# A decode-attention kernel: shorter TensorE program with hardware loops, z built by GpSimd, head sums by one masked product

## Chip, cores, metric

One core of one Trainium2 chip. The metric is the device time of one execution in microseconds; times quoted are medians of several runs. A span is the stretch from the first to the last instruction. It is 1.3 to 1.6 us shorter than the time in most of them and up to 2.8 us shorter in a few, so a single high time need not come from the kernel's own work.

## The reference, cut to what matters

Two token rows go through grouped-query attention on a long cache, a small gated feed-forward part, and an output projection:

```
x = layernorm(A_x)                                  # (2, 1, 512)
q = (x @ wq)                                        # 32 query heads of 128
p = softmax(q . k_cache * 128**-0.5)                # cache: 2 x 8 kv heads x 32768 x 128, bf16
s = (p . v_cache) @ wo                              # 4 query heads share a kv head
g = silu(mlp(x))                                    # weights w3, w4: 1.8 MB each
out = A_x + s * g
```

K and V are 268 MB of the 280.5 MB that are read, each byte once. A *group* below is one of the 16 pairs (batch row, kv head): 8.39 MB of K and as much of V. *z* is the small tile that holds a group's query heads among zeros; it is the stationary operand of the score products. *Heads* are a group's finished, normalized results.

## The kernel before

Loads go through one queue, in order (in the trace of before the seven pieces of the output weights are issued from 610.3 to 613.2 us, and land one after the other from 642.7 to 650.1 us). K of the next group is released when the first half of this group's scores is done, V when its weighted sum is done. Both signals come from one-column marker matmuls (`mark`) on TensorE.

```python
    with pe.Fori(0, NG):
        head_sums()                       # of the group before
        take(pe, s_z)
        for i in range(NPART):            # two halves, written out
            for r in range(NR):
                take(pe, s_t)             # transposed K from VectorE
                ... 4 matmuls of 512 columns into sc[i] ...
                mm.then_inc(s_tf if r < NR - 1 else s_sc, 1)
            mark(s_tf)
            if i == 0:
                mark(p_k)                 # releases the next K load
        ... sum of the exponentials ...
        for h in range(NPART):            # weighted sum of V, half by half
            take(pe, s_v[h], 16)
            ... 32 matmuls, four at a time (at 63.2 us of the trace four start within 0.01 us) ...
        mm.then_inc(s_o, 1)
        mark(p_o)                         # releases the next V load
```

The weighted sum lies in PSUM as 4 blocks of 128 columns, each valid for some rows. ScalarE copies it (`ob`), TensorE adds up the right rows, VectorE normalizes and picks the diagonal:

```python
        act.copy(out=ob[:, :], in_=o[:, :]).then_inc(s_ob, 1)
        ...
        for t in range(VT):               # head_sums: 4 products of 128 columns, fp32
            mm = pe.matmul(oT, lhsT=sel_o[:, t, ...], rhs=ob[:, t * Dh:(t + 1) * Dh], ...)
        ...
        dve.reciprocal(rec, S); dve.scalar_tensor_tensor(xm, oT, rec, mask); dve.tensor_reduce(...)   # cut
```

At the end the output weights come in seven pieces behind the last V. Rows of the first two pieces do not need the last heads (`early`), and their sum is copied out by ScalarE while the last heads are still being made:

```python
    early(0)
    head_sums()
    k_e = P(early(1))
    k_es = A(act.copy(out=e_sb[:, :], in_=e_ps[:, :]))
    pe.wait_ge(s_r, NG + 2)               # the last heads
    product(2)
    ... four products that add the early sums ...
    for i in range(3, len(WO_PARTS)):
        mm = product(i)
```

The softmax here doesn't subtract the row's maximum and nothing guards it: scores larger than these inputs give would overflow.

Of the kernel before, what the change touches and what calls it, by code (L numbers as in the profile page):

```python
# [15 lines left out]
RT = 16  # L16
# [5 lines left out]
WO_PARTS = [(0, 0, 8), (0, 8, 16), (1, 0, 8), (1, 8, 12), (1, 12, 14), (1, 14, 15), (1, 15, 16)]  # L22
# [38 lines left out]
def kernel(  # L61
# [63 lines left out]
    xm = sbuf([128, WL, RS], F32, "xm")  # L125
# [5 lines left out]
    sel_t = sbuf([128, VT, rep], F32, "sel_t")  # L131
    sel_o = sbuf([128, VT, NQ, rep, WL], F32, "sel_o")
    sel_u = sbuf([128, rep], F32, "sel_u")
    sel_h = sbuf([128, NQ, rep, WL], F32, "sel_h")
    mask = sbuf([128, WL], F32, "mask")
    x_bf = sbuf([128, D], BF16, "x_bf")
    xf, xn, ln2 = (Ts[0].bitcast(F32)[:, 0:D], Ts[0].bitcast(F32)[:, D:2 * D], Ts[1].bitcast(F32)[:, 0:D])
    xn_bf = sbuf([128, D], BF16, "xn_bf")
    ln2_bf = sbuf([128, D], BF16, "ln2_bf")
# [20 lines left out]
    banks = [nc.alloc_psum_tensor(f"bank{i}", [128, 512], F32) for i in range(8)]  # L160
    sc = banks[0:2]
    o, S_b, oT_b, h_ps, treg_b, s_b = banks[2:8]
    S = S_b[:, 0:1]
    oT = oT_b[:, 0:Dh]
    treg = treg_b[:, 0:2 * DK * 16].bitcast(BF16)
    h2, e_ps = o, sc[0]
    e_sb = Ts[2].bitcast(F32)[:, 0:D]
    mark_ps = treg_b[0:1, 0:1]
# [13 lines left out]
    end_p, end_v = pe.alloc_register("end_p"), dve.alloc_register("end_v")  # L182
    for eng, reg in ((pe, end_p), (dve, end_v)):
        eng.reg_mov(reg, 0)
    s_far = nc.alloc_semaphore("s_far")
    ahead = pe.mark_branch_hint_location()
    top = nc.cur_bb
    pe.br_lt(end_p, 0, on_true="late", on_false="go").branch_hint(ahead)
    nc.switch_bb("go")
    hint_p, hint_v = pe.mark_branch_hint_location(), dve.mark_branch_hint_location()  # L190
    hints = [i.name for i in top.bb.instructions if isinstance(i, mybir.InstBranchHint)]
    begin(nc, first.ins.name, *hints)
# [6 lines left out]
    s_t, s_tf, s_z, s_sc, s_e, s_p, s_o, s_ob, s_x, s_on, s_d, s_r, p_k, p_o = (  # L199
        nc.alloc_semaphore(n)  # L200
        for n in ("s_t", "s_tf", "s_z", "s_sc", "s_e", "s_p", "s_o", "s_ob", "s_x", "s_on", "s_d", "s_r", "p_k",
                  "p_o")
# [49 lines left out]

    k_x0 = V(dve.memset(x_bf[:, :], 0.0))
# [9 lines left out]
    k_id = G(  # L263
# [4 lines left out]
    )  # L268
    G(pool.memset(ones_f[:, :], 1.0))
# [9 lines left out]
    V(dve.memset(s_ps, 0.0))  # L279
    V(dve.memset(o[:, :], 0.0))  # L280
    V(dve.memset(S, 1.0))
    V(dve.memset(oX[:, :], 0.0))
    V(dve.memset(h_bf[:, :, :], 0.0))
    k_t0 = V(dve.memset(xT[:, :, :], 0.0))
# [25 lines left out]
    k_xb = V(dve.tensor_copy(out=xn_bf[0:BW, :], in_=xn[0:BW, :]))  # L310
    k_l2 = layernorm(1, ln2, xn, k_xn)
    wait(dve, k_l2)
    k_lb = V(dve.tensor_copy(out=ln2_bf[0:BW, :], in_=ln2[0:BW, :]))
# [9 lines left out]
    wait(pe, k_id)  # L323
    for s, (src, k_src) in enumerate(((xn_bf, k_xb), (ln2_bf, k_lb))):
        wait(pe, k_src)
        for k in range(DK):
            c = (s * DK + k) * 32
            k_tr = P(pe.transpose(out=treg[:, c:c + BW], in_=src[0:BW, k::DK], identity=ident[0:BW, 0:BW]))  # L328

    wait(dve, k_id)  # L330
    V(
        dve.tensor_reduce(
            out=sel_t[:, :, :],
            in_=ident[:, :].rearrange("p (j a t h) -> p a t h j", j=4, t=VT, h=rep)[:, 0, :, :, :],
            axis=AX.X, op=ALU.add,
# [9 lines left out]
            out=mask[:, :], in_=ident[:, :].rearrange("p (j w) -> p w j", w=WL), axis=AX.X, op=ALU.add  # L345
# [9 lines left out]
    wait(dve, k_tr, k_t0)  # L355
    k_xT = V(
        dve.tensor_copy(out=xT[:, :, 0:B], in_=treg.rearrange("p (k c) -> p k c", c=32)[:, :, 0:BW:BS])
    )

    wait(pool, k_sh, (g_, g_.n))  # L360
    G(pool.tensor_copy(out=sel_h[:, :, :, :], in_=wide(sel_u[:, :], WL)))
    for t in range(VT):
        wait(pool, (g_, g_.n))
        G(pool.tensor_copy(out=sel_o[:, t, :, :, :], in_=wide(sel_t[:, t, :], WL)))
# [9 lines left out]
    for t in range(NQB):  # L374
        for k in range(DK):
            for n in range(NQ):
                c = (t * NQ + n) * GW
                i = pe.matmul(
                    sc[t][32 * n:32 * n + 32, :], lhsT=xT[:, k, :],
                    rhs=wq3[:, k, c:c + GW].rearrange("p (h w e) -> p h e w", h=rep * NB, e=2),  # L380
                    start=(k == 0), stop=(k == DK - 1), tile_position=(0, 32 * n),
                )
        k_q.append(P(i))
# [9 lines left out]
    def spread(eng, j, n):  # L393
        return (eng.copy if eng is act else eng.tensor_copy)(
            out=qr[32 * j:32 * j + 32, :, :, :].rearrange("p a e (m n h) -> p (a e) m n h", n=NQ, h=rep)[
                :, :, :, n, :
            ],
            in_=qT[32 * n:32 * n + 32, 0:B, :].rearrange("p b (t h a) -> p a (b t) h", t=NQB, h=rep),
        )

    wait(act, k_qT)
    wait(pool, k_qT, (g_, g_.n))
    for n in range(NQ):
        for j in range(NQ):
            if n < 2 or j < 2:
                k_qa = A(spread(act, j, n))
            else:
                k_qg = G(spread(pool, j, n))
# [3 lines left out]
    w4v = w34[:, W4O:W4O + FK * D].rearrange("p (f d) -> p f d", f=FK)  # L412
    HW = 32 * FK
    wait(pe, k_w3)
    for k in range(DK):
        for n in range(NQ):
            i = pe.matmul(
                h_ps[32 * n:32 * n + 32, 0:HW], lhsT=xT[:, DK + k, :], rhs=w3v[:, k, n * HW:(n + 1) * HW],
                start=(k == 0), stop=(k == DK - 1), tile_position=(0, 32 * n),
            )  # L420
    k_h = P(i)
    wait(dve, k_h)
    k = V(
        dve.transpose(
            out=hT[:, :, :], in_=h_ps[:, 0:HW].rearrange("p (q f) -> p f q", f=FK),
        )
    )
    hf = hT[:, :, 0:B]
# [19 lines left out]
    k_hb = V(dve.tensor_mul(out=h_bf[:, :, 0:BW:BS], in0=hf, in1=th[:, :, :]))  # L448
    wait(pe, k_hb, k_w4)
    for f in range(FK):  # L450
        i = pe.matmul(h2[0:32, :], lhsT=h_bf[:, f, :], rhs=w4v[:, f, :], start=(f == 0), stop=(f == FK - 1))  # L451
    k_h2 = P(i)
# [13 lines left out]
    for m in range(1, NG):  # L466
        sp.wait_ge(p_k, m)
# [9 lines left out]
    wait(act, k_z0, k_qa, k_qg)  # L477
    act.sem_inc(s_ob, 1)
    with act.Fori(0, NG) as m:
        for j in range(4):  # L480
            c = (NR - 1) * rep + 32 * j
            i = act.copy(  # L482
                out=z[32 * j:32 * j + 32, :, :, c:c + rep],
                in_=qr[32 * j:32 * j + 32, :, :, bass.ds(m * rep, rep)],
            )
        i.then_inc(s_z, 1)
        for i in range(NPART):
            take(act, s_sc)
            act.activation(  # L489
# [3 lines left out]
        act.copy(out=ob[:, :], in_=o[:, :]).then_inc(s_ob, 1)  # L493
# [8 lines left out]
    sel = sel_h[:, :, :, :].rearrange("p j h w -> p (j h w)")  # L502

    def group(odd):
        hs = halves(odd)
        for i in range(NPART):
# [3 lines left out]
            for r in range(NR):  # L510
                take(dve, s_tf)
# [4 lines left out]
        for i in range(NPART):  # L516
            h = hs[i]
            take(dve, s_e)
            if i == 0:
                dve.tensor_scalar_mul(out=sms[0][:, :], in0=sel, scalar1=rss[0][:, 0:1]).then_inc(s_d, 1)  # L520
# [4 lines left out]
            if i == 1:  # L525
                take(dve, s_d)
                dve.scalar_tensor_tensor(
                    out=sms[1][:, :], in0=sel, scalar=rss[1][:, 0:1], in1=sms[0][:, :], op0=ALU.mult, op1=ALU.add
                ).then_inc(s_p, 1)

    def heads(dst, p0):
# [4 lines left out]
                out=xm[p0:, :, :], in0=oT[p0:, :].rearrange("p (w r) -> p w r", w=WL), scalar=rec[p0:, 0:1],  # L536
                in1=mask[p0:, :].unsqueeze(2).to_broadcast([128 - p0, WL, RS]), op0=ALU.mult, op1=ALU.mult,
            )
        )
        with nc.allow_low_precision(reason="all terms but one are zero"):  # L540
            dve.tensor_reduce(  # L541
                out=dst, in_=xm[p0:, :, :].rearrange("p w r -> p r w"), axis=AX.X, op=ALU.add
# [3 lines left out]
    dve.sem_inc(s_tf, T_BUFS)  # L546
# [14 lines left out]
    def mark(sem):  # L561
        pe.matmul(mark_ps, lhsT=ident[:, 0:1], rhs=ident[:, 0:1], start=True, stop=True).then_inc(sem, 1)  # L562

    def head_sums():
        take(pe, s_ob)
        for t in range(VT):
            mm = pe.matmul(  # L567
                oT, lhsT=sel_o[:, t, :, :, :].rearrange("p j h w -> p (j h w)"),
                rhs=ob[:, t * Dh:(t + 1) * Dh], start=(t == 0), stop=(t == VT - 1),
            )  # L570
        mm.then_inc(s_x, 1)

    wait(pe, (g_, g_.n), (v_, v_.n))
    with pe.Fori(0, NG):
        head_sums()
        take(pe, s_z)
        for i in range(NPART):
            for r in range(NR):
                Tb = Ts[(NR * i + r) % T_BUFS][:, :].bitcast(BF16)
                Tb = Tb.rearrange("p (b c e) -> p b c e", b=NB, e=2)  # L580
                zc = (NR - 1 - r) * rep
                take(pe, s_t)
                for nb in range(NB):
                    for e in range(2):
                        mm = pe.matmul(  # L585
                            sc[i][:, :], lhsT=z[:, nb, e, zc:zc + 128], rhs=Tb[:, nb, :, e],
                            start=(r == 0 and nb == 0 and e == 0),
                            stop=(r == NR - 1 and nb == NB - 1 and e == 1),
                        )
                mm.then_inc(s_tf if r < NR - 1 else s_sc, 1)  # L590
            mark(s_tf)
            if i == 0:
                mark(p_k)
        take(pe, s_p)
        pe.matmul(S, lhsT=sms[1][:, :], rhs=ones_f[:, 0:1], start=True, stop=True)  # L595
        for h in range(NPART):
            take(pe, s_v[h], 16)
            vt = vbuf[:, h * SLOT:(h + 1) * SLOT].rearrange("p (t d) -> p t d", d=Dh)
# [108 lines left out]
```

## Time and profile before

| | before |
|---|---|
| time, median of three runs (lowest to highest) | 654.38 us (654.26 to 655.57) |
| span | 652.8 us |
| read | 280.50 MB, 430 GB/s over the span |
| busy: TensorE, VectorE, ScalarE | 59%, 53%, 12% |
| time before the first packet; after the last landing | 1.0 us; 2.7 us |

No engine is busy for over 59% of the span, and the DMA share is 1.00 from 41.5 to 640 us. An engine's work can cost time in two places only: where it lets the load queue run dry, and after the last bytes. The prediction below shows the lines.

### The profile page before, as it was taken

The page shows a single profiled execution, that of the slowest core. Times are in us where ns is not written, and L with a number is a line of the kernel's source. Part 1 is how long each engine was busy: PE and PEld are TensorE (multiplying, and loading weights), DVE is VectorE, ACT ScalarE, POOL GpSimd, SP SyncE. Part 2 cuts the span into 40 slices and gives each one's busy share as a digit, 9 for nine tenths or more (in the row PEclk, how much of TensorE's full clock was granted, in tenths as well). Part 3 has the DMA queues.
Part 4 walks back from the last instruction along what each step waited for, and adds up shares of the span by engine and source line. Part 5 has one row for each costly group of instructions (what it writes and reads, how often), then busy time and mean ns, then how long its engine had stood idle before and what let it go on. Part 6 is the DMA issues. An engine that isn't in the chain of part 4 may idle for free. (4 is left out here: it accounts for less than half of the span.)

```text
span 652.8 us, 6524 instructions
## 1 busy us (share of the span) xinstructions
PE 386.2 (59%) x2406; PEld 156.5 (24%) x2438; DVE 346.0 (53%) x412; ACT 76.7 (12%) x184; POOL 7.7 (1%) x29
## 2 busy tenths in 40 slices
PE   0548195672828658293764829367383945828785
PEld 0113132230313213131221213123121322212332
DVE  4257191753809266391835629174481926539570
ACT  1320102020010201101020010201001020010100
POOL 3100000000000000000000000000000000000000
PEclk9769688695978859697786878878697896869798
DMA  9999999999999999999999999999999999999997
GB/s 386 475 396 448 446 446 410 434 446 450 414 426 446 450 422 418 446 450 422 418 446 450 430 410 450 446 438 402 450 446 446 398 446 446 446 406 434 426 442 294
DMA packets 6506, 280.53 MB, mean 430 GB/s; under 512 B 736, under 2 KB 1000, under 8 KB 1256
## 3 DMA queue, kind: packets, MB, share of 16 engines
q1 hardware_dynamic: 6492, 280.50, 99.4%
q8 instruction: 1, 0.02, 0.0%
q10 hardware_dynamic: 12, 0.01, 0.0%
q14 instruction: 1, 0.01, 0.0%
HBM read 280.50 MB, written 0.00 MB: 430 GB/s over the span
## 5 line engine op out<-in xcount | busy, mean ns | idle before, releaser
L585 PE MATMUL bank<-T,z 128*128 128x512 bf16 x992 | 272.6, 422 | 189.7 <-PEq L46 184.9
L512 DVE STREAM_TRANSPOSE T<-kbuf 128x1024 int32<-128x1024 int32 x256 | 290.7, 1211 | 130.5 <-DVEq L46 130.5
L585 PEld LDWEIGHTS bank<-T,z 128*128 128x128 bf16 x1024 | 97.4, 103 | 352.1 <-issue 274.9
L602 PE MATMUL bank<-vbuf,pt 128*16 128x512 bf16 x1024 | 73.0, 449 | 2.5 <-PEq L46 2.5
L489 ACT ACTIVATE ep<-bank 128x512 bf16<-128x512 f32 x32 | 19.1, 598 | 438.5 <-ACTq L46 438.5
L533 DVE RECIPROCAL rec<-bank 128x1 f32<-128x1 f32 (+1 forms) x17 | 2.9, 169 | 118.8 <-DVEq L46 118.8
L602 PEld LDWEIGHTS bank<-vbuf,pt 128*16 128x16 bf16 x1024 | 27.6, 102 | 39.7 <-issue 21.5
L521 DVE STREAM_TRANSPOSE pt<-ep 128x512 bf16<-128x512 bf16 x32 | 22.9, 715 | 22.0 <-DVEq L46 22.0
L567 PE MATMUL bank<-ob,sel_o 128*128 128x128 f32 x136 | 19.7, 289 | 16.4 <-PEq L46 16.4
L595 PE MATMUL bank<-ones_f,sm 128*128 128x1 f32 x32 | 6.2, 264 | 31.3 <-PEq L46 31.3
L567 PEld LDWEIGHTS bank<-ob,sel_o 128*128 128x128 f32 x136 | 16.9, 196 | 21.8 <-issue 21.8
L493 ACT COPY ob<-bank 128x512 f32<-128x512 f32 x16 | 9.4, 587 | 102.6 <-ACTq L46 102.6
L482 ACT ACT_TABLE_LOAD x16 | 20.5, 1283 | 0.3
L595 PEld LDWEIGHTS bank<-ones_f,sm 128*128 128x128 f32 x32 | 5.3, 210 | 32.2 <-issue 32.2
L482 ACT COPY z<-qr 32x16 bf16 x64 | 13.0, 202 | 0.7
L451 PE MATMUL bank<-vbuf,h_bf 128*32 128x512 bf16 x14 | 4.9, 523 | 6.2 <-DVE h_bf L448 6.2
L562 PE MATMUL bank<-ident 128*1 128x1 bf16 x64 | 8.4, 165 | 0.0
L328 PE MATMUL bank<-ident,xn_bf 17*128 17x17 bf16 x4 | 0.3, 177 | 13.1 <-POOL x L319 13.1
L562 PEld LDWEIGHTS bank<-ident 128*1 128x1 bf16 x64 | 4.0, 82 | 16.2 <-issue 14.4
L541 DVE TENSOR_REDUCE oA<-xm 128x128 f32 x16 | 5.9, 366 | 3.8 <-DVEq L46 3.8
L535 DVE SCALAR_TENSOR_TENSOR xm<-bank,rec,mask 128x128 f32<-128x128 f32 (+1 forms) x17 | 6.0, 351 | 2.5 <-DVEq L46 0.2
L489 ACT ACTIVATION_READ_ACCUMULATOR ep<-bank 128x1 f32 x32 | 6.4, 200 | 0.2
(75 smaller groups left out, 55.1 us busy)
## 6 DMA issues: line engine op xcount, KB each, us to landing
vbuf<-in_A_v_cache_dram SPq DMA_DIRECT2D x4, 4096.0 KB, 29.5
kbuf<-in_A_k_cache_dram SPq DMA_DIRECT2D x2, 4096.0 KB, 22.9
kbuf<-in_A_wq_dram SPq DMA_DIRECT2D x1, 4096.0 KB, 13.5
vbuf<-in_B_w_dram SPq DMA_DIRECT2D x2, 1792.0 KB, 18.2
kbuf<-in_A_wo_dram SPq DMA_DIRECT2D x3, 1024.0 KB, 34.4
kbuf<-in_A_wo_dram SPq DMA_DIRECT2D x1, 512.0 KB, 37.1
kbuf<-in_A_wo_dram SPq DMA_DIRECT2D x1, 256.0 KB, 37.3
kbuf<-in_A_wo_dram SPq DMA_DIRECT2D x2, 128.0 KB, 37.1
```

Of the source, the lines that this page charges most:

```text
L482: i = act.copy(out=z[32 * j:32 * j + 32, :, :, c:c + rep], in_=qr[32 * j:32 * j + 32, :, :, bass.ds(m * rep, rep)],)
L489: act.activation(out=eps_[i][:, :], in_=sc[i][:, :], func=ACT.Exp, scale=inv_sqrt_dh, accum_out=rss[i][:, :]).then_inc(s_e, 1)
L493: act.copy(out=ob[:, :], in_=o[:, :]).then_inc(s_ob, 1)
L512: dve.transpose(out=Ts[(NR * i + r) % T_BUFS][:, :].rearrange("p (b t k) -> p t b k", b=NB, t=RT), in_=kt[:, r * W:(r + 1) * W].rearrange( ...
L521: dve.transpose(out=pts[h][:, :, :].rearrange("p r (t h) -> p t r h", h=rep), in_=eps_[i][:, :].rearrange("p (t r h) -> p t r h", r=NR, h= ...
L535: dve.scalar_tensor_tensor(out=xm[p0:, :, :], in0=oT[p0:, :].rearrange("p (w r) -> p w r", w=WL), scalar=rec[p0:, 0:1], in1=mask[p0:, :].u ...
L541: dve.tensor_reduce(out=dst, in_=xm[p0:, :, :].rearrange("p w r -> p r w"), axis=AX.X, op=ALU.add).then_inc(s_r, 1)
L562: pe.matmul(mark_ps, lhsT=ident[:, 0:1], rhs=ident[:, 0:1], start=True, stop=True).then_inc(sem, 1)
L567: mm = pe.matmul(oT, lhsT=sel_o[:, t, :, :, :].rearrange("p j h w -> p (j h w)"), rhs=ob[:, t * Dh:(t + 1) * Dh], start=(t == 0), stop=(t ...
L585: mm = pe.matmul(sc[i][:, :], lhsT=z[:, nb, e, zc:zc + 128], rhs=Tb[:, nb, :, e], start=(r == 0 and nb == 0 and e == 0), stop=(r == NR - 1 ...
L595: pe.matmul(S, lhsT=sms[1][:, :], rhs=ones_f[:, 0:1], start=True, stop=True)
L602: mm = pe.matmul(o[32 * j:32 * j + VT * rep, :], lhsT=pts[h][:, r, a * VT * rep:(a + 1) * VT * rep], rhs=vt[:, u * VT:(u + 1) * VT, :].rea ...
```

## The change

Its intent is a TensorE program that fits in two instruction blocks, so that no third one has to be fetched (the fetches that the traces show during the run are packets of kind "instruction", of 16 and of 8 KiB). The two score halves become a loop with a register-addressed PSUM bank, the feed-forward part gets loops too, the markers go (ScalarE and GpSimd release the loads), z is built by GpSimd, and the head sums become one product on columns that ScalarE has masked. The order of the output projection is altered. The core of the diff, with cuts:

```diff
-WO_PARTS = [..., (1, 0, 8), (1, 8, 12), (1, 12, 14), (1, 14, 15), (1, 15, 16)]
+WO_PARTS = [..., (1, 0, 8), (1, 8, 11), (1, 11, 14), (1, 14, 15), (1, 15, 16)]
...
-        act.copy(out=ob[:, :], in_=o[:, :]).then_inc(s_ob, 1)
+        act.sem_inc(s_po, 1)                       # GpSimd passes it on to the V load
+        for t in range(VT):
+            w = slice(t * Dh, (t + 1) * Dh)
+            i = act.activation(out=ob[:, w], in_=o[:, w], func=ACT.Copy, scale=sel_t[:, t:t + 1])
+        i.then_inc(s_ob, 1)
...
-        for t in range(VT):
-            mm = pe.matmul(oT, lhsT=sel_o[:, t, ...], rhs=ob[:, t * Dh:(t + 1) * Dh], ...)
+        mm = pe.matmul(oT, lhsT=sel_h[...], rhs=ob[:, :], start=True, stop=True)   # 512 columns
...
+    with pool.Fori(0, NG) as m:
+        pool.tensor_tensor(out=zw, in0=qr[..., bass.ds(m * rep, rep)], in1=sel_j, op=ALU.mult).then_inc(s_z, 1)
+        take(pool, s_po)
+        pool.sem_inc(p_o, 1)
...
+    with pe.Fori(0, NPART) as i:
+        for r in range(NR):
+            ... sc2[:, bass.ds(i * 512, 512)] in place of sc[i] ...
...
     early(0)
-    head_sums()
-    k_e = P(early(1))
+    early(1)
+    pe.wait_ge(s_r, NG + 2)
+    early(2)
+    k_e = P(early(3))
     k_es = A(act.copy(out=e_sb[:, :], in_=e_ps[:, :]))
-    pe.wait_ge(s_r, NG + 2)
-    product(2)
+    product(4)
```

So the copy of the early sums now stands behind the last heads.

## The prediction

> **What bounds the kernel now.** I read the busy shares, the forty slices, the windows, the chain that ended last, the sync queue's waits, the loads' times to landing, and the timeline of one head group and of the tail. First the engines against the transfers, from the page.
>
> ```profile
> PE 386.2 (59%) x2406; PEld 156.5 (24%) x2438; DVE 346.0 (53%) x412; ACT 76.7 (12%) x184; POOL 7.7 (1%) x29
> ...
> DMA  9999999999999999999999999999999999999997
> GB/s 386 475 396 448 446 446 410 434 446 450 414 426 446 450 422 418 446 450 422 418 446 450 430 410 450 446 438 402 450 446 446 398 446 446 446 406 434 426 442 294
> ...
> HBM read 280.50 MB, written 0.00 MB: 430 GB/s over the span
> ```
>
> No engine is busy over 60% of the time, while the transfers are in the top tenth in every slice but the last. The windows (last two columns: DMA share and GB/s) show where they are not full.
>
> ```profile
> 0.00:1.00 1.00, 0.00 (x0) 0.00 (x0) 0.00 (x0) 0.00 (x0) 0.20 (x4) 1.00 0.00 0
> ...
> 41.50:640.00 598.50, 367.45 (x2199) 147.92 (x2231) 332.20 (x369) 64.05 (x154) 0.00 (x0) 0.82 1.00 434
> 640.00:649.00 9.00, 6.62 (x109) 3.47 (x113) 0.90 (x3) 1.17 (x2) 0.00 (x0) 0.81 0.95 391
> 649.00:650.20 1.20, 0.80 (x32) 0.31 (x24) 0.00 (x0) 0.00 (x0) 0.00 (x0) 1.00 0.04 15
> 650.20:652.80 2.60, 0.21 (x4) 0.07 (x4) 0.58 (x2) 0.00 (x0) 0.00 (x0) 0.78 0.00 1
> ```
>
> From 41.5 to 640 us the share is 1.00 at 434 GB/s, with no gap. 280.5 MB at 434 GB/s is 646.3 us. The span is 652.8, so everything that is not streaming costs 6.5 us: 1.0 us before the first packet, 2.6 us after the last landing, and some 3 us of slower small pieces, in the first 4 us and the last 10. The chain (start, us, what) says the same of the end.
>
> ```profile
> 613.16 36.97 DMA kbuf<-in_A_wo_dram
> 650.13 0.04 issue
> 650.18 0.26 PE bank L637 x4
> 650.44 0.02 issue
> 650.46 0.30 DVE sg L662
> 650.76 0.02 issue
> 650.79 0.29 DVE out L664
> ```
>
> The last output-weight piece is issued at 613 us, waits behind the last V in the same queue and lands at 650.13; only four small matmuls, two VectorE operations and the store follow.
>
> **How much room the engines have.** Engine work can matter only where it makes a load be issued after the queue has run dry. The loads of K and V take turns, 8.39 MB each, so each takes 8.39/434 = 19.3 us of queue. The times to landing, for the tile of K and then of V between 80 and 590 us:
>
> ```profile
> DMA to landing us min/median/max: 26.6/27.5/27.9
> DMA to landing us min/median/max: 30.6/30.8/32.3
> ```
>
> A load that took 19.3 us to move and landed 27.5 us after issue stood 8.2 us behind the other (7.3 at the least); V stood 11.5 us (11.3 at the least). These are the slacks. The timeline of one group shows what sets the issues: the K load follows the first half's scores, the V load follows the weighted sum of V.
>
> ```profile
> 90.47 0.19 PE L562 MATMUL bank<-ident 128*1 128x1 bf16 x2
> ...
> 90.70 0.33 SPq L235 DMA_DIRECT2D kbuf<-in_A_k_cache_dram  x1
> ...
> 106.98 0.17 PE L562 MATMUL bank<-ident 128*1 128x1 bf16 x1
> 107.23 0.33 SPq L235 DMA_DIRECT2D vbuf<-in_A_v_cache_dram  x1
> ```
>
> [...] The trace has only one 16 KiB and one 8 KiB packet of kind "instruction" after the start; 24 KB at 434 GB/s is 0.06 us of transfer, so there is almost nothing to win. [...]
>
> **The change part by part.**
> - TensorE, head group. Removed: four one-column marker matmuls per group (64 of 165 ns in all, 0.66 us a group). Head sums go from four products (8 records, 1.13 us in the timeline) to one of 512 columns; in the records one fp32 product of 128 columns is two, at 0.40 us for 8 or 0.05 us each [...], so 512 columns are an estimated 2 x 0.2 = 0.4 us plus one weight load of 2 x 0.2 us: 0.3 us saved. Added: [...] 64 matmuls that take their PSUM address from a register. I put the latter at 0 to 0.09 us each: ScalarE's four copies for z in before, which read at a register's offset, take 0.84 us for four of 0.202, so nothing shows between them; VectorE's reduction with a register's offset waits 0.24 us after its predecessor where the one without waits 0.15. Worst sum 64 x 0.09 = 5.8 us a group, 2.9 to the first half. Both are under 11.3 and 7.3, so off the path.
> - Loads' release. K's count now comes from ScalarE as it takes the scores, V's from ScalarE through GpSimd. I allow 0.1 and 0.3 us, against the slacks above. GpSimd's z (64 elements by 128 partitions; casts of 32x64 took 288 ns) is some 0.5 us, and has the whole weighted sum's shadow but not that of its own group: it runs after the release, beside ScalarE's copy and the head sums.
> - ScalarE. Lost: four z copies (0.84 us a group). One copy of 587 ns becomes four masked ones of 128 columns; from 255 ns for a 32x128 copy [...], 4 x 0.3 = 1.2 us (estimate). The table load (1.28 us, at the z copies now) may move in front of the exponential; its result is wanted only after both halves' transposes, some 7 us later. Off the path.
> - VectorE. Normalizing and reduction go from 128 to 512 columns, from 351 and 366 ns to an estimated 0.75 each at about 1 ns a column: 0.8 us a group in 16 us of idle. Off the path.
> - Start. Feed-forward part: 16 matmuls lose their four-way packing (1.2 to about 3 us), three more transposes of 0.65 us (2 us)[...]; 12 more GpSimd casts (3.5 us, beside that). Sum 5 to 8 us. It releases the second half of the first V, which was issued at 32.2 us while the queue was full to beyond 50 us, and lets the group loop begin at 40 to 43 instead of 35 us, with K landing at 41.5. A delay of the first scores by 2 us eats 2 of 8 us of slack. Off the path.
> - Tail. Nothing in the last two pieces changes. Before it: masked copies +0.6, head sums -0.3, normalizing and reduction +0.8, so the last heads are ready 1.1 us later, at 647.85 instead of 646.75. Then eleven packed rows (0.6 us; the piece they need lands at about 648.6), 0.75 us for the copy of the early sums, which now comes after the last heads and not beside them, and 0.4 to 0.8 us for its four products: 650.0 to 650.5. The last weights land at 650.13. So the tail grows by 0 to 0.4 us.
>
> Sum: 0 from the stream, 0 from the start, +0.2 us from the tail. 654.4 + 0.2 = **654.6 us**.
>
> **The rivals.**
> - *Register-addressed matmuls become the bound.* At c us more each, the V slack of 11.3 is gone at c = 0.18, K's 7.3 at 32c, c = 0.23. At 0.3 us: 64 x 0.3 - 11.3 = 7.9 us a group, times 15, 118 us: 773 us. Against it: the ScalarE copies above. For it: no matmul of before has such an address. I give it 2%.
> - *The transfer ring drains at the start*, because the feed-forward loops are far slower[...]. They would have to cost over 15 us beyond my estimate; then each further us adds one, 655 to 665 us. 1%.
> - *The tail is longer* because ScalarE's copy and the products with a half-rate clock stand behind the last landing: +1 to +1.5 us, 655.5 to 656. Likely enough to shape the upper edge, too small for 2% (13 us).
> - *Faster*, if the fetches removed had held up the stream. The share of 1.00 speaks against it; all of the non-streaming time is 6.5 us, 1%, so over 2% is out of reach.
>
> **Range and chances.** The three runs of before spread from 654.26 to 655.57; with -0.5 to +1.5 us of tail the range is 653.6 to 656.2. Faster by over 2%: 0.01; same: 0.97; slower: 0.02.
>
> **What would show it.** Right: DMA share 1.00 and 434 GB/s in the middle window; K and V landings shorter by the delay of the release but still above 19.3 us; marker matmuls gone; the chain still ending in the output weights' landing near 650 us. The tail step is right if TensorE waits less for the last weights and the end moves by under 0.5 us. Wrong: landing times near 19.3 us and a share below 0.99 in mid-span (first rival), a gap before 80 us (second), or a chain that ends in ScalarE's copy of the early sums (third).

What no trace or run of this case gave is cut from this text: a paragraph but for its count of the fetched packets, a stall at each fetch, what a loop's branch takes (in a head group and for the 12 loop turns at the start), and what the scale operand adds to a masked copy. The forecast as recorded came to 654.4 + 0.2 = 654.6 us. Of the cut terms only the last enters that sum: the 1.2 us for the masked copies and the tail's +0.6 were estimated with it. With the 255 ns of a plain copy alone they would be 4 x 0.255 = 1.0 and +0.4 us, the last heads 0.9 in place of 1.1 us later, and the forecast 0.2 us lower at most (an estimate from these numbers). At the start the sum of 5 to 8 us lies within the slack and adds nothing to the forecast.

The trace of before shows what three other figures rest on. VectorE took 546 ns for 512 columns (L302) and 1211 ns for 1024 (L512), so about 1 ns a column. Two rows of four packed products of 448 columns start 0.19 us apart (at 20.27 and 20.46 us), so 16 one after the other come to about 3 us (an estimate). And the granted clock is 0.50 in some stretches, from 24 to 30 us for one, and 1.00 in others: that is the half rate of the third rival.

## The result

| | before | changed |
|---|---|---|
| time, median of 6 runs (lowest to highest) | 654.38 us (654.12 to 655.57) | 655.62 us (655.15 to 655.9) |
| span of the profiled run | 652.8 us | 653.8 us |

The ratio is 1.0014, 95% interval 1.0001 to 1.0027. Ratios here are the mean time of one kernel's runs over the mean of the other's runs of the same rounds, so not quite the ratio of the medians. By the 2% rule this is "same", and the time lies inside the range; but it is about 1 us more. The spans separate the kernels better than the times: 653.7 to 654.5 us in the six runs of the changed kernel, 652.7 to 653.5 in the 29 runs of the kernel before. The traces say where the difference lies.

The page of the changed kernel, its slices and its reads:

```profile
DMA  9999999999999999999999999999999999999996
...
HBM read 280.50 MB, written 0.00 MB: 429 GB/s over the span
```

Its windows, with the columns as before (clock, DMA share, GB/s last):

```profile
41.50:640.00 598.50, 367.43 (x2047) 134.87 (x2078) 350.30 (x372) 59.63 (x140) 4.39 (x15) 0.82 1.00 434
640.00:649.00 9.00, 6.49 (x50) 1.87 (x50) 1.59 (x3) 1.14 (x4) 0.00 (x0) 0.62 0.96 395
```

The stream is the same: share 1.00, 434 GB/s. The times to landing of K and of V between 80 and 590 us in the changed kernel:

```profile
DMA to landing us min/median/max: 26.5/27.2/27.8
DMA to landing us min/median/max: 30.2/30.3/31.9
```

They are 0.3 and 0.5 us shorter than before: the loads are issued that much later and still stand in the queue for 8 and 11 us, so nothing is lost. The stream ends as before too (in the semaphore marks of the trace, the last weights are complete at 650.13 us before and 650.25 us after). The chain that ended last is another one:

```profile
648.34 1.01 DVE oX L546
649.35 0.04 issue
649.40 0.85 PE ps L631 x11
...
650.27 0.59 ACT T L656
...
650.91 0.41 PE ps L660 x8
651.32 0.13 PE ps L643 x8
```

Before, it ended in the landing of the weights. Now it comes from VectorE's last reduction, through eleven rows of early sums, their copy and their addition. At 650.25 us the last weights are there, and the copy has only begun. VectorE's last two operations start at 651.47 in place of 650.46, and that 1.0 us is the whole difference of the spans.

Why are the last heads late? The tail in the timeline of before (start, us, engine, line, operation):

```profile
640.34 2.61 PE L602 MATMUL bank<-vbuf,pt 128*16 128x512 bf16 x32 [2.54 <-PEq L46]
...
643.06 0.59 ACT L493 COPY ob<-bank 128x512 f32<-128x512 f32 x1 [10.22 <-ACTq L46]
643.79 1.63 PE L567 MATMUL bank<-ob,sel_o 128*128 128x128 f32 x8
...
646.39 0.36 DVE L541 TENSOR_REDUCE oX<-xm 32x16 bf16<-32x128 f32 x1
```

and of the changed kernel:

```profile
640.48 2.95 PE L606 MATMUL ps<-vbuf,pt 128*16 128x512 bf16 x32 [3.10 <-PEq L46]
643.63 1.14 ACT L482 ACTIVATE ob<-ps,sel_t 128x128 f32<-128x128 f32 x4 [9.68 <-ACTq L46]
644.92 2.04 PE L569 MATMUL ps<-ob,sel_h 128*128 128x512 f32 x2 [1.49 <-PEq L46]
...
648.34 1.00 DVE L546 TENSOR_REDUCE oX<-xm 32x16 bf16<-32x512 f32 x1
```

The heads are ready at 649.34 in place of 646.75: 2.6 us later. Of these, 0.57 us are the later start of ScalarE's copy (the second half of the weighted sum took 0.34 us longer, 2.95 for 2.61; the rest is its later start and a slightly longer way to ScalarE); 0.55 us are the copies (1.14 for 0.59); 0.41 us the head sums (2.04 for 1.63); 1.05 us VectorE (from its first operation to its last, 2.23 for 1.18). Before had 3.4 us between the heads and the landing, and one part of that was already a wait for a piece of the weights; the changed kernel has 0.9.

The clock column goes with two of these terms, the longer half and the head sums: in the window from 640 to 649 us it is 0.62 in the changed kernel and 0.81 before. In the changed kernel's trace the head sums of the earlier groups take 1.10 us (at 71.3 and at 609.9 us the clock is 1.00), and those of the tail take 2.04 with the clock at 0.50. The tail of before was slowed too, but less: 1.63 us, with the clock at 0.69, for head sums that take 1.13 in its earlier groups (at 108.0 us the clock is 1.00).

### The profile page after: what moved, and what is told of

It is laid out like the page before. It is cut to its first block, busy times and chain, and to the rows that moved or that the text cites. A ratio compares the mean times of both kernels' runs of the same rounds, so it can differ in the third digit from the quotient of the medians.

```text
span 653.8 us, 6483 instructions
## 1 busy us (share of the span) xinstructions
PE 391.5 (60%) x2200; PEld 142.1 (22%) x2232; DVE 370.8 (57%) x419; ACT 67.2 (10%) x156; POOL 14.9 (2%) x56
## 5 line engine op out<-in xcount | busy, mean ns | idle before, releaser
L592 PE MATMUL ps<-T,z 128*128 128x512 bf16 x992 | 276.5, 424 | 170.8 <-PEq L46 165.5
L592 PEld LDWEIGHTS ps<-T,z 128*128 128x128 bf16 x1024 | 98.9, 104 | 354.1 <-issue 275.2
L606 PE MATMUL ps<-vbuf,pt 128*16 128x512 bf16 x1024 | 72.4, 446 | 3.1 <-PEq L46 3.1
L569 PE MATMUL ps<-ob,sel_h 128*128 128x512 f32 x34 | 20.5, 688 | 27.3 <-PEq L46 27.3
L606 PEld LDWEIGHTS ps<-vbuf,pt 128*16 128x16 bf16 x1024 | 27.5, 101 | 39.8 <-issue 21.7
L475 ACT ACTIVATE ep<-ps 128x512 bf16<-128x512 f32 x32 | 19.1, 597 | 103.1 <-ACTq L46 102.9
L482 ACT ACTIVATE ob<-ps,sel_t 128x128 f32<-128x128 f32 x64 | 18.2, 367 | 103.5 <-ACTq L46 103.5
L546 DVE TENSOR_REDUCE oA<-xm 128x512 f32 x16 | 16.1, 1005 | 3.8 <-DVEq L46 3.8
L540 DVE SCALAR_TENSOR_TENSOR xm<-ps,rec,mask 128x512 f32<-128x512 f32 (+1 forms) x17 | 12.8, 751 | 2.5
L441 PE MATMUL ps<-vbuf,h_bf 128*32 x12 | 7.2, 606 | 0.4
```

Of the source, the lines that this page charges most:

```text
L441: pe.matmul(h2[0:32, :], lhsT=h_bf[:, bass.ds(f, 1), :].rearrange("p f c -> p (f c)"), rhs=w4v[:, bass.ds(f, 1), :].rearrange("p f d -> p ...
L475: act.activation(out=eps_[i][:, :], in_=sc[i][:, :], func=ACT.Exp, scale=inv_sqrt_dh, accum_out=rss[i][:, :]).then_inc(s_e, 1)
L482: i = act.activation(out=ob[:, w], in_=o[:, w], func=ACT.Copy, scale=sel_t[:, t:t + 1])
L540: dve.scalar_tensor_tensor(out=xm[p0:, :, :], in0=oT[p0:, :].rearrange("p (q r) -> p q r", r=RS), scalar=rec[p0:, 0:1], in1=mask[p0:, :, : ...
L546: dve.tensor_reduce(out=dst, in_=xm[p0:, :, :].rearrange("p q r -> p r q"), axis=AX.X, op=ALU.add).then_inc(s_r, 1)
L569: mm = pe.matmul(oT, lhsT=sel_h[:, :, :, :].rearrange("p j h w -> p (j h w)"), rhs=ob[:, :], start=True, stop=True)
```

## The experiments

Three theories: **T**, the tail is all of it; **S**, the stream is slower or later; **P**, the loops and branches of the TensorE program cost it.

### Only the tail order put back

```diff
 # on the changed kernel
+WO_PARTS, early() and product() as before; the copy of the early sums ahead of the last heads
```

> The changed kernel with only the order of the output projection put back: the early sums cover the first two pieces and the rest goes through the per-row products, as in the kernel before. Theory T (the whole +1.2 us is the tail after the last V: the last heads come 2.6 us later, and the copy of the early sums then stands behind them): the heads stay at 649.3 us of the span, but after them stand some 1.5 us of products in place of 2.1 us of sums, copy and products, so 0.3 to 0.6 us less than the changed kernel, 655.1 us; the chain that ended last still starts at the last reduction. Rival S (the stream itself is slower or later): no change, 655.6 us, and the chain ends in the landing of the output weights.

Measured: 654.77 us against 654.47 of before, ratio 1.0003 (0.999 to 1.0017). The chain ends in the landing of the weights, not in the reduction as T had it. In this profile the clock in the tail was 1.00 from 640.4 to 650 us: the second half of the weighted sum took 1.90 us and the heads were ready at 647.6, so the trace does not show what the order does to late heads. One of the five runs has a span of 654.2 us, as long as the changed kernel's; it has no profile, so whether its heads were late is not known.

### Only the head sums put back

```diff
 # on the changed kernel
-masked copies, one product of 512 columns, 512 columns on VectorE
+one copy, four products of 128 columns, 128 columns on VectorE
```

> The changed kernel with only the head sums put back: one plain ScalarE copy, four products of 128 columns, normalizing and reduction over 128 columns. Loops, two blocks and the GpSimd z stay. Theory T: the last heads are ready at about 647 us again, the tail's end is set by the landing of the last weights at 650.2 us or by the copy of the early sums (within 0.3 us of it), so 654.4 to 654.7 us. Rival S or a rival P (the loops and branches of the TensorE program cost the time): stays at 655.6 us.

Measured: 654.50 us, ratio 1.0004 (0.999 to 1.0017). Its last reduction, and the landing in its chain:

```profile
647.38 0.37 DVE L547 TENSOR_REDUCE oX<-xm 32x16 bf16<-32x128 f32 x1
```

```profile
611.40 38.23 DMA kbuf<-in_A_wo_dram
```

Heads are ready at 647.75 us although the clock was low here too (0.63 from 640.4 to 643.5 us and 0.50 from there to 647; second half 2.95 us); the chain ends in the landing. T's number; P and S fall short, as loops and releases are all still in it.

### Both put back

```diff
 # on the changed kernel: the two edits above together
```

> The changed kernel with both put back, head sums and tail order; what is left of the change is the TensorE program in loops, the GpSimd z, the release of the loads by ScalarE and GpSimd, and the start. Theory T: equal to the kernel before within 0.2 us, 654.4 us, with the chain ending in the landing of the output weights. Rival P (loops, branches): 655.6 us.

Measured: 654.21 us, ratio 0.9999 (0.9985 to 1.0012), the chain ending in the landing. The median span is 652.9 us, that of the kernel before 652.9. Loops, branches, GpSimd's z and the start cost nothing that can be seen: P falls.

### The kernel before with the new head sums

```diff
 # on the kernel before
-one copy, four products of 128 columns, 128 columns on VectorE
+masked copies, one product of 512 columns, 512 columns on VectorE
```

> The kernel before with only the head sums changed to the masked copies, one product and 512 columns. Theory T: the last heads are ready at 649 to 649.4 us, then the products of the old tail order of some 1.5 us: ends about 0.6 to 0.9 us later than the kernel before, 655.0 to 655.3 us, and about equal to the changed kernel with the old tail order. Rivals S and P: no change, 654.4 us.

Measured: 654.27 us, ratio 0.9998 (0.9984 to 1.0012). T missed: no cost that can be seen. Its timeline and its chain:

```profile
647.91 1.00 DVE L540 TENSOR_REDUCE oX<-xm 32x16 bf16<-32x512 f32 x1
```

```profile
613.51 36.97 DMA kbuf<-in_A_wo_dram
```

The heads are as late as 648.9 us, 2.2 later than in before, and still the chain ends in the landing, at 650.48 in this run. What follows them is shorter than I had reckoned: 32 products in 0.62 us, the addition of the early sums that were copied long before, and the rest waits for the weights anyway. So heads at 648.9 us are not late enough in the old order. But the room left was small: TensorE worked on without a longer pause until 650.18, and the last weights landed 0.35 us later than in before, so some 0.3 us later would have shown (an estimate from this timeline). What the order changes is how late the heads may be. From the heads to the end of the last product the changed kernel needs 2.1 us (649.34 to 651.45). Its weights are there at 650.25 and take some 0.3 us of products more, so heads after about 648.4 us end the chain (an estimate from these traces). Measured back from each run's last landing, the old order leaves the heads some 0.5 us more. Heads as late as the changed kernel's, 649.34, would by this estimate cost something in the old order too, only less. So the loss needs late heads, and the copy behind them uses up the room sooner.

### The changed kernel again, and with work in the pause

The second call repeated the changed kernel, and gave TensorE work in its wait for the last half of V, to see whether that half then takes less time.

> The changed kernel once more, unchanged, so that it stands beside the kernel before and the variants on one chip. In the four variants the TensorE clock in the tail differed by profile (second half of the last weighted sum 1.90 us in two, 2.95 and 3.31 us in the others), and neither part put back alone left the chain on the last heads. Theory T2: the 1.2 us needs three things together, heads later by their longer work, the early sums' copy behind the heads, and a half-rate clock in the tail. Then this kernel is at 655.6 us wherever the second half takes about 2.95 us and the head sums 2.04 us, and at 654.4 to 654.9 us where the clock is full.

Measured: 654.98 us against 654.20, ratio 1.0008 (0.9995 to 1.0021): a little over half of the first difference, in medians 0.8 us, and the interval includes 1. The spans are 653.1 to 653.7 us (median 653.5) against 652.7 to 653.5 (652.8) for before. The trace shows the same chain again, beginning at

```profile
647.92 1.01 DVE oX L546
```

with a second half of 3.41 us, head sums of 1.10, and a span of 653.7.

```diff
 # a_warm, on the changed kernel, in every group
+        if h == 1: 13 x pe.matmul(mark_b, lhsT=ident, rhs=vbuf[:, 0:512])   # unread bank
```

> The changed kernel with 13 extra matmuls of 512 columns into an unread bank ahead of the second half of each weighted sum (correct result), so that TensorE doesn't pause while it waits for the last V. Theory T2: the second half then takes 1.9 us and the head sums 1.1 us, the last heads are ready at 647.4 to 647.9 us, the chain ends in the landing of the last weights, 654.4 to 654.7 us; the extra 2.8 us a group fall into the V loads' slack of 11 us and change nothing else. Rival D (the longer VectorE and ScalarE work and the copy behind the heads cost it at any clock): 655.3 to 655.6 us. Rival S (the stream): 655.6 us.

Measured: 656.08 us, ratio 1.003 (1.0018 to 1.0042). This one was badly built: in the profiled run, the slowest of six at 660.15 us, the last group's second exponential starts at 638.6 us, against 633.3 in the changed kernel, so the second half of the weighted sum began at 647.2 instead of 640.5, and took 1.90 us. The 13 extra matmuls took 2.98 us in the last group. The extra work in every group had put the whole tail off, and the run tells nothing of the loss. The repair has 12 such matmuls in the last group only:

```diff
 # a_warm_last, on the changed kernel
+        if h == 1:
+            pe.br_lt(turn, NG, on_true="rest", on_false="warm")
+            ... block "warm": 12 x pe.matmul(mark_b, lhsT=ident, rhs=vbuf[:, 0:512]) ...
```

> The changed kernel with 12 extra matmuls of 512 columns into an unread bank, now by a branch in the last group only, between the two halves of its weighted sum, where TensorE waits 3 us for the last V. (a_warm had them in every group and pushed the last group's scores back by 6 us, so it told nothing of the clock.) Theory T2 (the half-rate clock in the tail is a part of the loss): second half 1.9 us instead of 2.95 to 3.4, heads ready about 1.3 us earlier, at 647.6 us; the chain then ends in the landing or within 0.4 us of it: 654.2 to 654.6 us. Rival D (the work behind the heads costs it at any clock): the chain still ends in the heads, 654.9 to 655.6 us.

Measured: 654.35 us against 654.27, ratio 1.0005 (0.9991 to 1.0019); one of five runs at 655.73, but with a span of 652.9. The timeline and the chain:

```profile
640.92 1.90 PE L614 MATMUL ps<-vbuf,pt 128*16 128x512 bf16 x32
...
644.32 1.10 PE L569 MATMUL ps<-ob,sel_h 128*128 128x512 f32 x2 [1.50 <-PEq L46]
...
646.79 1.00 DVE L546 TENSOR_REDUCE oX<-xm 32x16 bf16<-32x512 f32 x1
```

```profile
612.55 37.08 DMA kbuf<-in_A_wo_dram
```

With useless work in the pause, the same program has its heads 1.55 us earlier (647.79) and ends in the landing. So, as far as one profile and five runs tell, the slower TensorE work in the tail (2.95 and 2.04 us in place of 1.90 and 1.10) is the third part of the loss: without it the heads of the same program come before the limit of about 648.4 us. That this is the low clock rests on the other traces: the clock is 0.63 and 0.50 where the changed kernel does this work (640.4 to 643.5 and 643.5 to 647 us), and 1.00 from 640.4 to 643.5 us in the two profiles whose same half took 1.90 us (tail order put back, both put back).

One profile does not show that the useless work kept the clock up, for the clock was also 1.00 without it in two others. But the eight other profiles with all bytes and no added work agree with it. In six of them TensorE waited 2.54 to 4.09 us for the last half of V, and that half then took 2.61 to 3.41 us; in the other two it waited 0.49 and 2.41 us, and the half took 1.90. Here the pause of 2.63 us was filled, and the half took 1.90.

### Is one instruction fetch worth anything?

The changed kernel was meant to save a fetch, but its page shows two packets of 16 KiB of kind "instruction" (before: one), one of them in the stream, at 71.0 us (after the first group's weighted sum, which ends at 69.75, and before its head sums), and one at 652 us, when all data is there. In before the one comes at 5.6 us.

```diff
 # b_fill, on the kernel before, ahead of the head loop
+    pe.br_lt(end_p, 0, on_true="fill", on_false="heads")     # never taken
+    ... block "fill": 330 matmuls ...
```

> The kernel before with 330 matmuls that are never executed laid into the TensorE program ahead of the head loop, with a branch over them: no work is added, but the program is about 660 instructions longer and some further 16 KiB blocks must be fetched. In the records of both kernels the one such fetch in the stream takes 0.92 to 0.93 us on one of the 16 transfer engines, and from then on the last of the 16 landing marks of each load comes 0.9 us behind the others (from 5.6 us on in before, from 71 us on in the changed kernel). Theory F: a fetch holds one engine back to the end, so every further fetch within the stream lands the last weights 0.9 us later if it falls on the same engine: with two to four more fetches 1.8 to 3.7 us, 656 to 658 us, with 434 GB/s as before. Rival (a fetch costs its bytes only, 0.04 us of all engines, or falls on different engines): 654.4 to 655.3 us.

Measured: 654.46 us against 654.27, ratio 1.0005 (0.9991 to 1.0019). The page:

```profile
q8 instruction: 3, 0.05, 0.0%
```

Two more fetches did occur (at 32.2 and 39.4 us), and the time did not grow: F's number did not come. The landing marks (the semaphore updates of the transfer engines in the trace) suggest why: of the last V's first half, 13 of 16 marks came by 639.2 us and three between 640.1 and 640.3. In before, with one fetch, 15 came by 639.3 us and one at 640.2. This fits each fetch having fallen on another transfer engine and held that one back by about 0.9 us, so that the last of 16 was no later than with one fetch. What two fetches on one engine would do was not tested.

### What the change does to the engines themselves

With half of the K and V bytes (wrong result) the stream no longer hides the engines.

```diff
-    if m < last: load all of dst
+    if 0 < m < last: load the first half of each slot of dst
```

`h_before` and `h_after` are the two kernels with this edit. `h_after_heads` adds the old head sums (the edit of the second run above), `h_after_static` this:

```diff
 # on the changed kernel with half bytes
-    with pe.Fori(0, NPART) as i:  ...  sc2[:, bass.ds(i * 512, 512)]
+    for i in range(NPART):        ...  sc[i]
```

> The kernel before with half the bytes: groups 1 to 14 load only the first half of each slot of K and V, so the result is wrong on purpose; instructions and waits are the same. This takes the stream off the path and shows the engines' own period. In the trace of before one group from the first transpose to the end of the heads takes 30.4 us (80.15 to 110.56). Theory: about 30 us a group in place of 38.6, so 16 x 30 + 41 + about 20 at the end = 530 to 550 us. If engine work set the pace already in the full kernel it would stay near 654 us.

> The changed kernel with the same half bytes (wrong on purpose). Here what the change does to the engines must show, since no stream hides it. Theory: the serial chain of a group gains 0.55 us of masked copies and 1.05 us of normalizing and reduction, and loses some 0.7 us of markers, branches and load releases: 30.4 + 0.3 to 0.9 us a group, so 5 to 14 us slower than h_before, 540 to 560 us. Rival L (the loops save time on the engines): 5 us or more faster than h_before.

> Half bytes (wrong on purpose), the changed kernel with the old head sums. h_before ran 526.9, h_after 543.8 us. Theory: of the 16.9 us some 2.6 us are the later start of the group loop, and the rest is the longer serial chain from the weighted sum to the next transposes: masked copies 0.55 and VectorE 1.05 us a group, 1.6 x 15 = 24 us, less what the new form saves. So about 520 to 530 us, at h_before or below. Rival L (the loops, the register addresses and the releases by ScalarE and GpSimd cost it): stays at 538 to 544 us.

> Half bytes (wrong on purpose), the changed kernel with the two turns of the score loop written out and the banks addressed without a register. Theory: a register address costs nothing on TensorE (mean matmul of 424 ns in the changed kernel against 422), the loop's branch some 0.1 to 0.25 us a group: 540 to 544 us. Rival 1 of the prediction (register-addressed matmuls slow): well under 540 us.

| half bytes | time, us | first K transpose of group 0, of group 15, us | us a group | to the end, us |
|---|---|---|---|---|
| before | 526.92 | 41.5, 491.0 | 29.97 | 34.2 |
| changed | 543.78 | 45.0, 506.3 | 30.75 | 36.0 |
| changed, old head sums | 537.02 | 44.3, 501.5 | 30.48 | 35.1 |
| changed, score loop written out | 546.19 | 44.4, 505.0 | 30.70 | 35.8 |

The middle of the span in before and in the changed kernel, at half bytes:

```profile
80.00:480.00 400.00, 322.27 (x1889) 123.36 (x1887) 279.27 (x310) 54.88 (x132) 0.00 (x0) 0.90 0.69 280
```

```profile
80.00:480.00 400.00, 298.09 (x1720) 110.61 (x1719) 285.21 (x301) 49.43 (x117) 3.82 (x13) 0.89 0.68 274
```

The DMA share is 0.69 and 0.68, so these runs do show the engines. The changed kernel is slower by 17.0 us of span: 3.5 at the start, 11.7 over fifteen groups, 1.8 at the end. I had expected 5 to 14, and for the old head sums a return to 520 to 530 us; they gave back only 4.1 of the 11.7: a miss for both expectations. The rest belongs to the program form, the releases or the clock, which these runs do not separate: one weighted sum of the same 64 products (near 304 us) took 5.32 us in before, and those of the changed kernel took 3.63, while over the whole span the clock of before was the higher one (0.893 against 0.882). What they do answer is the rival of the register addresses: written out with fixed banks, the score loop is not faster (542.9 to 548.6 us in four runs). And 30.7 us a group against the stream's 38.6 is why 0.8 us a group costs nothing in the real kernel.

No variant beat the kernel before by more than the intervals.

## Why the prediction was right, and where not

**The bound: right.** The stream sets the time. From the first transpose of group 1 to that of group 14 a group took 38.6 us in both kernels, with 434 GB/s in both.

**The slacks: right.** Later releases only shortened the times to landing, as said.

**Register addresses: right.** I allowed 0 to 0.09 us a matmul. The score rows of before and of the changed kernel (count, busy us, mean ns of one):

```profile
L585 PE MATMUL bank<-T,z 128*128 128x512 bf16 x992 | 272.6, 422 | 189.7 <-PEq L46 184.9
```

```profile
L592 PE MATMUL ps<-T,z 128*128 128x512 bf16 x992 | 276.5, 424 | 170.8 <-PEq L46 165.5
```

422 and 424 ns. The address is put in a register once a turn.

**The branches: measured, not predicted.** The trace of before does show them, when asked for the source line of a loop: 16 of 79 to 242 ns on TensorE's head loop (L574, median 220). In the changed kernel a group has one of 71 ns (L581), two of about 144 (L584) and one of 177 (L614, medians), together 0.3 us more than before.

**The start: right in size.** The group loop's first transpose came at 44.15 instead of 41.50 us, within the slack. GpSimd's z took 0.29 us (I said 0.5), the masked copies 1.14 (1.2, the estimate), and the table load (1.28 us) did move in front of the exponential.

**The tail: the parts right in kind, the sum too small, and so the wrong end of the chain.** By the signs that I had set, this step failed: the chain was to end in the landing with the end moved by under 0.5 us; it ended in the last reduction and the early sums' copy, and the end moved by 1.0 us. The term that was mis-sized is the lateness of the last heads: I had 1.1 us, it was 2.6.
- *Head sums "-0.3"*: +0.41. I took 0.05 us for an fp32 product of 128 columns from a group of eight in 0.40 us. Those eight run four at a time (in the trace four start within 0.02 us, with the clock at 1.00); the products of the head sums start one by one, 0.11 us apart. My own line of 1.13 us for the four products of before would have said so. One of 512 columns takes 1.10 us with the clock at 1.00, no less than the four of before (1.13), and took 2.04 with it at 0.50.
- *Normalizing and reduction "+0.8"*: +1.05. Normalizing was right (0.75); the reduction over 512 columns takes 1.00, not 0.75.
- *Weighted sum: not in my list*: the copy after it starts 0.57 us later, 0.34 of it from the longer half (clock 0.63 against 0.70 before).
- *Copy behind the heads*: right, and it took the room that the late heads would have had in the old order. The result is what my third rival described, 655.5 to 656 us, with the half-rate clock as one of its parts (0.50 from 643.5 to 647 us). That the time still lies inside the range is owed to this rival, which had set the upper edge. The range is not the sum that I gave for it, though: 654.26 - 0.5 to 655.57 + 1.5 is 653.8 to 657.1, not 653.6 to 656.2.

**The fetches: right outcome, wrong sum.** I divided 24 KB by the rate of all engines and got 0.06 us. In the traces the 16 KiB packet takes 0.93 us in before (at 5.6 us) and 0.92 us in the changed kernel (at 71.0 us), and after it one of the 16 landing marks of each load comes about 0.9 us behind the others, to the end of the stream. Whether a program with no fetch in the stream would land the last weights 0.9 us earlier stays open: none was run.

What also stays open is the size of the loss: 1.24 us in medians in the first rounds and 0.8 in the second, which ran on chip 7. The clock in the tail differs between the two profiles (head sums 2.04 and 1.10 us); that this makes the difference is not shown.

## What to carry to other kernels

When a kernel's transfers never pause (here a DMA share of 1.00 at 434 GB/s), compare new engine work with the slack of each load and then look only at what stands behind the last byte; most of this rewrite cost and gained nothing. Behind the last byte the order counts as well as the work: a copy that waits for the last result can turn a delay that had room into one that does not. And give the work there the durations that it has in the tail of a trace, not those of mid-stream: after its wait for the last V, TensorE took 1.90 us for the same half of the weighted sum in two profiles and 2.61 to 3.41 us in six.
